# A fused attention and feed-forward kernel: batch 2 loaded ahead of w_out, batch 1's attention given priority, the last unit stored by column halves

## The chip, the cores and the metric

The kernel runs on one core of one Trainium2 chip. The metric is the device time of one execution in microseconds (us); a kernel is given by the median of its runs. PE is TensorE, DVE is VectorE, ACT is ScalarE, POOL is GpSimd, SP is SyncE. Spans that are read from a profile are some 2 us shorter than the device time of the same run, and belong to a single run, so they are used for where the time goes, and the timed rounds for how much it is.

## The reference, cut to what matters

```python
batch, n_heads, seq, head_dim = (8, 8, 576, 64)      # q, k, v: float32
kv  = np.einsum('bhsd,bhse->bhde', k, v)
out = np.einsum('bhsd,bhde->bhse', q, kv)
rms = np.sqrt(np.mean(out * out, axis=-1, keepdims=True) + 1e-06)
x   = (out / rms * g_norm) -> [4608 tokens, 512]
y   = ((x @ w_a) * (x @ w_b)) @ w_out                # d_ff 1536, y: [4608, 512]
```

The attention has no softmax: a 64x64 matrix per head, applied to q, then a norm. The feed-forward part is nearly all of the work. The kernel computes in 16 bit and, except for the first 512 tokens, saves one product in eight by a scheme of sums and differences of blocks (seven products in place of eight). That saves PE time and costs DVE time, for the sums.

## The kernel before

The program is written as a list of nodes, each with an engine, an estimated duration, a priority and its dependencies. A small planner in the program itself orders the nodes when the program is built; the order that it finds on each engine is then fixed. So a number in the program is often not a wait on the chip but a guess that steers the order ("plan time", which is not quite the time of the trace).

```python
class Plan:
    def order(self):
        ...
                    t = max(self.ready(n), f)
                    key = (f if t < f + 0.06 else t, n.prio)   # what can start first, then priority
        ...
```

Every batch's attention is eight slices of a chain PE, ACT, PE, ACT, DVE: x = kvd'q (L344), square (L354), mean by a matrix of ones (L358, the "s" matmul), 1/root (L362), multiply into the 16-bit tokens `xp` (L367). Four stretches of it, shortened (`...` marks a cut):

```python
    # loads: weights, then w_out, then (load_node) batch 2, 3, ...; all casting loads, issued by POOL
    for i, (f0, f1) in enumerate(WB):
        nc.gpsimd.dma_start(out=wa_t[:, :, sl], in_=wa_v[:, :, sl])
        nc.gpsimd.dma_start(out=wb_t[:, :, sl], in_=wb_v[:, :, sl])
        ...                                              # batch 1 in between
    for i in range(2):
        nc.gpsimd.dma_start(out=wo_t[:, sl, :], in_=wo_v[:, sl, :])

    def load_node(b, prio, dep):     # batch b; q goes to DRAM in bf16 and comes back transposed
        def issue():
            if dep is not None:      # POOL waits here for the transposed q of the batch before
                nc.gpsimd.tensor_copy(gate_t, dep["q"].tile[0:1, 0, 0:1])
            ... q -> scr, k -> k_t, v -> v_t
        def transpose():
            nc.sync.dma_start_transpose(out=ld["q"].tile[:]..., in_=scr[:]...)
```

```python
    def o_std(ab, muls, win):        # w_out for the first 512 tokens: no sums, so no DVE
        for g in range(ng):          # 4 row groups of 128 tokens
            def mm(g=g, ps=ps):
                for fc in range(FC):                       # 12 products of 512 columns
                    nc.tensor.matmul(ps.tile[:], lhsT=ab.tile[:, fc, ...], rhs=wo_t[:, fc, :], ...)
            n1 = plan.add("PE", mm_us(FC, d_model), pr, mm, [plan.at(46.5)] + list(muls.values()), [ps], [ab])
```

```python
    # the last unit of 512 tokens (in o_unit); X, Z, W are PSUM banks, ob is the output tile
            ...
            p7 = prod(4, X, sx(s3), t3, False, [e2, n3], (), [s3], 0)
            ...
            c22 = comb(4, 1, 1, X, [p7, e5], [X, u5], u=u5)
            p3 = prod(5, Z, sx(s4), b22, False, [e5, n4], (), [s4], 3)
            c12 = comb(5, 0, 1, Z, [p3, e2], [Z])
            for i in range(m):
                put(0, slice(i, i + 1), [c11, c12], queue=("SP", "ACT")[i])
            for i in range(m):
                subs = slice(i, i + 1)
                p4 = prod(6 + 0.1 * i, W[i], a22, t4, True, [n4], [W[i]], subs=subs)
                c21 = comb(6 + 0.1 * i, 1, 0, W[i], [p4, e3], [W[i]], subs)
                put(1, subs, [c21, c22], queue=("ACT", "SP")[i])
```

Of the kernel before, what the change touches and what calls it, by code (L numbers as in the profile page):

```python
# [135 lines left out]
def kernel(  # L136
# [39 lines left out]
    NMAX = N0 // 2  # L176
    nb = len(BLOCKS)
    NJ = FC // 2
    EH = d_model // 2

    const = ctx.enter_context(tc.tile_pool(name="const", bufs=1))
# [106 lines left out]
    for i, (f0, f1) in enumerate(WB):  # L288
# [2 lines left out]
        nc.gpsimd.dma_start(out=wb_t[:, :, sl], in_=wb_v[:, :, sl])  # L291
        if i in (2, 4):
            early_load(early[1], 1, slice((i // 2 - 1) * HP, i // 2 * HP))
    for i in range(2):
        sl = slice(i * FC // 2, (i + 1) * FC // 2)
        nc.gpsimd.dma_start(out=wo_t[:, sl, :], in_=wo_v[:, sl, :])


    def dummies(n):
# [212 lines left out]
    def late_batch(b, load, win):  # L512
        at = Attn(b)
        w0, w1 = win
        kb, vb, qb = load["k"], load["v"], load["q"]
        kd = Buf(RKD)
        at.qt = [qb, kd]

        def view(t):
            return t[:, 0 : H * (NCH + 1) * D].rearrange("p (h c d) -> p h c d", h=H, d=D)  # L520

        s = Buf(RS)

        def kv_mm():
            kv_ps = s.tile[:].rearrange("p (a e) -> p a e", a=NP)
            for c in range(NCH + 1):
                for p in range(NP):
                    hs = slice(2 * p, 2 * p + 2)
                    nc.tensor.matmul(  # L529
                        kv_ps[:, p, :],  # L530
                        lhsT=kb.tile[:, c, hs, :],
                        rhs=view(vb.tile)[:, hs, c, :],
                        start=(c == 0 and p == 0),
                        stop=(c == NCH and p == NP - 1),
                    )

        n = plan.add(
            "PE", 1.15, w0, kv_mm, [(load["n"], load["kv_us"]), plan.at(w0 - 3)], [s, kd], [kb, vb]
        )

        def kv_out():
            kv_ps = s.tile[:].rearrange("p (a e) -> p a e", a=NP)
            at.kvd = kd.tile
            nc.scalar.copy(at.kvd[0:D, :, 0:D], kv_ps[0:D, :, 0:D])
            nc.scalar.copy(at.kvd[D:, :, D:], kv_ps[D:, :, D:])
            for p in range(NP):
                at.q[p] = qb.tile[:, p, :]

        m = plan.add("ACT", 0.75, w0, kv_out, [n], (), [s])
        slices(at, (w0 + 0.12 * (w1 - w0), w1), lambda p: [m, (load["qn"], 5.5)])  # L550


    def load_node(b, prio, dep):
        ld = {"k": Buf(RK), "v": Buf(RV), "q": Buf(RQT)}
        scr = scr_pool.tile([NP, S, 2, D], BF16, name="scr", tag="scr")

        def issue():
            if dep is not None:
                nc.gpsimd.tensor_copy(gate_t, dep["q"].tile[0:1, 0, 0:1])
            qv = q[b].rearrange("(p hl) s d -> hl s p d", hl=2)  # L560
            for hl in range(2):
                nc.gpsimd.dma_start(
                    out=scr[:, :, hl, :].rearrange("p s d -> s p d"), in_=qv[hl]
                )
            kt = ld["k"].tile
            ks = k[b, :, 0:SA, :].rearrange("h (sp c) d -> sp h c d", c=NCH)
            for c in range(NCH):
                nc.gpsimd.dma_start(out=kt[:, c], in_=ks[:, :, c, :])  # L568
            nc.gpsimd.dma_start(out=kt[0:SB, NCH], in_=k[b, :, SA:S, :].rearrange("h sp d -> sp h d"))
            for n, src in (("v", v),):  # L570
                t = ld[n].tile[:, 0 : H * (NCH + 1) * D].rearrange(
                    "p (h c d) -> p h c d", h=H, d=D
                )
                nc.gpsimd.dma_start(
                    out=t[:, :, 0:NCH, :],
                    in_=src[b, :, 0:SA, :].rearrange("h (sp c) d -> sp h c d", c=NCH),
                )
                nc.gpsimd.dma_start(
                    out=t[0:SB, :, NCH, :], in_=src[b, :, SA:S, :].rearrange("h sp d -> sp h d")
                )  # L580

        def transpose():
            nc.sync.dma_start_transpose(
                out=ld["q"].tile[:].rearrange("p a s -> p (a s)"),
                in_=scr[:].rearrange("a s h d -> (a s) (h d)"),
            )

        issue_us, q_us, ld["kv_us"] = (18.0, 8.0, 18.0) if dep is None else (9.0, 1.5, 11.5)

        ld["n"] = plan.add(  # L590
            "POOL", issue_us, prio, issue, [(dep["qn"], 5.5)] if dep else [], [ld["k"], ld["v"]]
        )
        ld["qn"] = plan.add(
            "SP", 2.5, prio, transpose, [(ld["n"], q_us)], [ld["q"]]
        )
        return ld

    gate_t = const.tile([1, 1], BF16)


    def std_block(win):
# [65 lines left out]
    def out_sums(prio):  # L667
        add, sub = nc.vector.tensor_add, nc.vector.tensor_sub
        b11, b12 = wo_t[:, 0:NJ, 0:EH], wo_t[:, 0:NJ, EH:]
        b21, b22 = wo_t[:, NJ:, 0:EH], wo_t[:, NJ:, EH:]  # L670
        t2, t3, t4 = (so_t[:, i] for i in range(3))
        n3, n1, n2, n4 = four(
            prio,
            fast_us(NJ * EH),
            ((t3, b22, b12, sub), (b12, b12, b11, sub), (t2, b22, b12, sub), (t4, b21, t2, sub)),
            [plan.at(46.5)],
            list(o_reads),
        )
        return n1, n2, n3, n4
# [106 lines left out]
            muls[j] = muls[j + NJ] = m  # L786
        return ab, muls

    def store(g0, o_sb, queue=None):
        queue = queue or nc.sync  # L790
        i = 0
        while i < 128:
            b, j = divmod(g0 + i, S)
            if b < NE:
                c, sp = divmod(j, EP)
                n = min(128 - i, EP - sp)
                r0, st = b * S + EC * sp + c, EC
            else:
                n = min(128 - i, S - j)
                r0, st = b * S + j, 1  # L800
            queue.dma_start(out=out[r0 : r0 + st * (n - 1) + 1 : st, :], in_=o_sb[i : i + n, :])
            i += n

    def o_block(bi, ab, muls, osum, win, chunks, rings, pieces):
# [15 lines left out]
    def o_std(ab, muls, win):  # L820
# [3 lines left out]
        for g in range(ng):  # L824
            pr = w0 + (w1 - w0) * g / ng
            ps = Buf((RO, RY)[g % 2])

            def mm(g=g, ps=ps):
                for fc in range(FC):
                    nc.tensor.matmul(  # L830
                        ps.tile[:],
                        lhsT=ab.tile[:, fc, g * 128 : (g + 1) * 128],
                        rhs=wo_t[:, fc, :],
                        start=(fc == 0),
                        stop=(fc == FC - 1),
                    )

            n1 = plan.add(
                "PE", mm_us(FC, d_model), pr, mm,
                [plan.at(46.5)] + list(muls.values()), [ps], [ab],  # L840
            )
            o_reads.append(n1)
            n2 = plan.add(
                "ACT", act_us(d_model), pr,
# [8 lines left out]
    def o_unit(r0, ab, muls, osum, pr, du, chunks, pieces, m, w, first, second, X, Y, Z, ob, s2, s3, s4, W):  # L853
# [81 lines left out]
                "DVE", dve_us((subs.stop - subs.start) * EH), pr + off * du, add, deps, (), frees  # L935
            )

        def put(fi, subs, deps, us=0.45, queue="SP"):
            q = {"SP": nc.sync, "ACT": nc.scalar}[queue]

            def go():
                for i in range(subs.start, subs.stop):
                    store(r0 + (fi * m + i) * 128, ob.tile[:, fi * m + i], q)

            plan.add(queue, us * (subs.stop - subs.start), pr + 7 * du, go, deps, (), [ob])

# [4 lines left out]
        if W:  # L951
# [14 lines left out]
            c22 = comb(4, 1, 1, X, [p7, e5], [X, u5], u=u5)  # L966
            p3 = prod(5, Z, sx(s4), b22, False, [e5, n4], (), [s4], 3)
            c12 = comb(5, 0, 1, Z, [p3, e2], [Z])
            for i in range(m):
                put(0, slice(i, i + 1), [c11, c12], queue=("SP", "ACT")[i])  # L970
            for i in range(m):
                subs = slice(i, i + 1)
                p4 = prod(6 + 0.1 * i, W[i], a22, t4, True, [n4], [W[i]], subs=subs)
                c21 = comb(6 + 0.1 * i, 1, 0, W[i], [p4, e3], [W[i]], subs)
                put(1, subs, [c21, c22], queue=("ACT", "SP")[i])
            return
        p1 = prod(0, X, a11, b11, True, [plan.at(46.5)], [X])
        e1 = ev(0, 0, 0, p1, [ob])
        p2 = prod(1, Y, a12, b21, True, [], [Y])
        c11 = comb(1, 0, 0, Y, [p2, e1], [Y])  # L980
# [18 lines left out]
    for i in range(len(lens)):  # L999
        st.append(st[-1] + lens[i] + (o_us[i - 1] if i else 0) + late_us * n_at[i])  # L1000
    L = [st[i + 1] - st[i] for i in range(len(lens))]
    at_win = {1: (34.5, st[1] - 3)}
    for b in range(2, B):
        t = b * S / N0
        at_win[b] = (max(61.0, st[int(t) - 1] + (t % 1) * L[int(t) - 1] - 18), st[int(t)] - 22 + (t % 1) * 12)
    loads = {2: load_node(2, 22.5, None)}
    for b in range(3, B):
        loads[b] = load_node(b, at_win[b - 1][0], loads[b - 1])
    early_batch(0, (4.0, 16.0))
    early_batch(1, at_win[1])  # L1010
    ab, muls, reads = std_block((st[0], st[1]))
    wsum = weight_sums(32.5, reads)
    needs = {1: [], 2: [2], 3: [3], 4: [4], 5: [5], 6: [6], 7: [7], 8: []}
    O_A, O_B = 12.0, 3.0
    for bi in range(1, nb + 1):
        o_win = (st[bi] + 1.0, st[bi + 1] - 1.0) if bi < nb else (st[bi] + O_A, st[bi + 1] + O_B)
        if bi == 1:
            o_std(ab, muls, o_win)
            osum = out_sums(st[2] - 10)
        else:  # L1020
            o_block(bi - 1, ab, muls, osum, o_win, 2, (RO, RY, RY), 1)
# [43 lines left out]
```

## Time and profile before

306.51 us, median of 4 runs (306.22 to 306.73).

| in the profiled run | us |
|---|---|
| first matmul of the feed-forward part starts | 19.9 |
| PE time lost between there and the last matmul | 3.66 |
| last matmul ends | 299.3 |
| span ends | 305.0 |

How the loss is read: back-to-back groups in the timeline show 0.216 us for a matmul of 512 columns, 0.109 for 256, 0.122 for 288. The distance between two starts less this is time in which PE did nothing. "PE busy" itself is no good for this, because the ends of matmuls are modelled. Read so, a total is good to about 0.1 us and that of one stretch to about 0.2 us. The loss sits in two places: 2.85 us between 35 and 50 us, 0.89 us between 70 and 90 us.

The stage table of the kernel before (stretch in us, its length, then the busy time of PE, PEld, DVE, ACT and POOL with instruction counts, PE's clock, DMA share and GB/s):

```profile
35.00:50.00 15.00, 13.00 (x107) 6.95 (x106) 12.65 (x26) 10.20 (x25) 7.36 (x8) 1.00 1.61 191
50.00:70.00 20.00, 20.00 (x148) 13.40 (x146) 13.17 (x23) 10.51 (x23) 8.92 (x10) 1.00 1.67 178
70.00:90.00 20.00, 19.66 (x184) 16.88 (x183) 19.93 (x40) 17.85 (x41) 10.01 (x12) 1.00 1.51 125
90.00:290.00 200.00, 200.00 (x1865) 178.84 (x1864) 168.09 (x303) 134.90 (x272) 28.11 (x30) 1.00 0.59 77
```

PE is what limits. DVE is idle for a third of 50 to 70 us and full from 70 to 90 us. The timeline of PE, kernel before, at the two places where it stops between 35 and 50 us (start, length, engine, line, what; the bracket is the idle time before it and what ended it):

```profile
37.12 0.28 PE L358 MATMUL bk<-sq,ones 128*128 128x288 bf16 x1 [0.65 <-ACT kvd L326]
37.99 0.28 PE L358 MATMUL bk<-sq,ones 128*128 128x288 bf16 x1 [0.59 <-ACT rs L362]
...
49.76 0.28 PE L358 MATMUL bk<-sq,ones 128*128 128x288 bf16 x1 [0.70 <-ACT rs L362]
```

All three are s matmuls of batch 1's attention, which stand in the order at a place where nothing else is left to run while ACT works. The timeline of POOL and that of SP's queue show the loads (lines of the kernel before: w_out's second half, batch 2's first, the gate that waits for batch 2's transposed q, and the transposing DMA itself):

```profile
31.23 0.82 POOL L296 DMA_DIRECT2D wo_t<-in_moe_w_out_dram  x1 [0.59 <-DMA abt<-in_q_dram]
32.73 1.65 POOL L562 DMA_DIRECT2D scr<-in_q_dram  x1 [0.68 <-DMA abt<-in_k_dram]
...
61.14 0.68 POOL L559 COPY gate_t<-qT 1x1 bf16<-1x1 bf16 x1 [11.08 <-DMA qT<-scr]
```

```profile
51.04 6.27 SPq L583 DMA_TRANSPOSE qT<-scr  x1
```

The end, from the timeline of the kernel before:

```profile
297.80 1.47 PE L894 MATMUL bk<-wo_t,as 128*128 128x256 f16 x12
298.62 0.69 DVE L932 TENSOR_TENSOR o_sb<-bk,u 128x512 f32<-128x512 f32 x1 [3.80 <-ACT o_sb L926]
299.23 1.34 DVE L932 TENSOR_TENSOR o_sb<-bk,o_sb 128x256 f32<-128x256 f32 x3
299.73 1.25 ACTq L801 DMA_DIRECT2D out_dram<-o_sb  x2
```

The last matmul ends at 297.80 + 1.47 = 299.27 us. The last product is the one on s4, whose combination is 512 columns wide, and it stands behind three others on DVE; then the last of four stores of 256 KB are issued. These four were issued from 299.7 to 300.6 us (the line of the stores, kernel before, from 299 to 304 us):

```profile
DMA to landing us min/median/max: 2.1/2.8/3.3
```

From the last matmul to the end of the span ("the tail" below) it takes 5.7 us.

### The profile page before, as it was taken

The page shows a single profiled execution, that of the slowest core. Times are in us where ns is not written, and L with a number is a line of the kernel's source. Part 1 is how long each engine was busy: PE and PEld are TensorE (multiplying, and loading weights), DVE is VectorE, ACT ScalarE, POOL GpSimd, SP SyncE. Part 2 cuts the span into 40 slices and gives each one's busy share as a digit, 9 for nine tenths or more (in the row PEclk, how much of TensorE's full clock was granted, in tenths as well). Part 3 has the DMA queues.
Part 4 walks back from the last instruction along what each step waited for, and adds up shares of the span by engine and source line. Part 5 has one row for each costly group of instructions (what it writes and reads, how often), then busy time and mean ns, then how long its engine had stood idle before and what let it go on. Part 6 is the DMA issues. An engine that isn't in the chain of part 4 may idle for free.

```text
span 305.0 us, 6667 instructions
## 1 busy us (share of the span) xinstructions
PE 292.3 (96%) x2621; PEld 239.2 (78%) x2621; DVE 235.0 (77%) x433; ACT 193.1 (63%) x404; POOL 77.0 (25%) x93
## 2 busy tenths in 40 slices
PE   7699899999999999999999999999999999999992
PEld 2444445498788898888988898899888888888881
DVE  4344678569998879698969986998599949898652
ACT  3584456279897768775688548965797466655520
POOL 8565742092480751914700000000000000000000
PEclk9689999999999999999999999999999999999999
DMA  7999999999799699999964400030004001100133
GB/s 188 210 198 198 198 207 158 194 178 166 79 139 170 42 161 229 116 168 201 143 77 80 138 3 0 2 140 1 2 0 140 1 2 69 72 3 0 36 104 138
DMA packets 98815, 33.16 MB, mean 109 GB/s; under 512 B 76768, under 2 KB 94176, under 8 KB 98784
## 3 DMA queue, kind: packets, MB, share of 16 engines
q0 software_dynamic: 77984, 17.99, 63.1%
q1 hardware_dynamic: 20096, 13.64, 18.8%
q10 hardware_dynamic: 704, 1.11, 1.2%
q8 instruction: 20, 0.33, 0.4%
q14 instruction: 11, 0.09, 0.1%
HBM read 37.75 MB, written 12.98 MB: 166 GB/s over the span
## 4 chain that ended last, share of the span: by engine, by line
PE 90%; DVE 4%; DMA 3%; ACT 1%; SPq 0%; issue 0%; DVEq 0%
PE bk L729 47%; PE bk L894 24%; PE bk L378 7%; PE bk L830 3%; DMA c<-in_v_dram 3%; PE bk L358 3%; PE bk L344 2%; PE bk L529 2%; PE bk L316 1%; DVE c L748 1%; DVE o_sb L932 1%; PE bk L332 1%; ACT rs L362 0%; PE bk L302 0%; DVE abt L393 0%; DVE xp L367 0%
## 5 line engine op out<-in xcount | busy, mean ns | idle before, releaser
L748 DVE TENSOR_TENSOR c<-bk,u 128x512 f16<-128x512 f32 x144 | 96.7, 686 | 27.1 <-PE bk L729 13.2
L411 ACT COPY u<-bk 128x512 f32<-128x512 f32 x144 | 82.2, 591 | 37.4 <-PE bk L729 36.4
L729 PE MATMUL bk<-xp,wa_t 128*128 128x256 f16 x288 | 55.0, 273 | 0.0
L729 PE MATMUL bk<-xp,wb_t 128*128 128x256 f16 x288 | 55.0, 273 | 0.0
L729 PEld LDWEIGHTS <-wa_t 128*128 128x128 f16 x384 | 37.4, 98 | 5.2
L894 PEld LDWEIGHTS <-abt 128*128 128x128 f16 x384 | 37.5, 98 | 4.8 <-DVE abt L783 0.2
L367 DVE SCALAR_TENSOR_TENSOR xp<-bk,g_col,rs 128x288 f16<-128x288 f32 x64 | 32.6, 512 | 11.2 <-ACT rs L362 11.0
L729 PEld LDWEIGHTS <-wb_t 128*128 128x128 f16 x384 | 37.6, 98 | 4.3
L411 ACT CAST c<-bk 128x512 f16<-128x512 f32 x48 | 28.4, 591 | 17.1 <-PE bk L729 16.6
L894 PE MATMUL bk<-wo_t,abt 128*128 128x256 f16 x288 | 37.0, 273 | 0.0
L729 PE MATMUL bk<-T,sa 128*128 128x256 f16 x192 | 36.6, 273 | 0.1
L729 PE MATMUL bk<-T,sb 128*128 128x256 f16 x192 | 36.6, 273 | 0.0
L362 ACT ACTIVATE rs<-bk,eps_t 128x288 f32<-128x288 f32 x64 | 32.5, 509 | 3.5 <-PE bk L358 3.2
L783 DVE TENSOR_TENSOR abt<-c 128x1024 f16<-128x1024 f16 x48 | 32.9, 686 | 1.7
L729 PEld LDWEIGHTS <-sa 128*128 128x128 f16 x288 | 28.1, 98 | 4.4 <-issue 0.7
L894 PEld LDWEIGHTS <-as 128*128 128x128 f16 x288 | 28.2, 98 | 3.4
L729 PEld LDWEIGHTS <-sb 128*128 128x128 f16 x288 | 28.2, 98 | 3.3
L354 ACT ACTIVATE sq<-bk 128x288 bf16<-128x288 f32 x64 | 25.5, 414 | 2.3 <-PE bk L344 2.0
L926 ACT COPY o_sb<-bk 128x512 f32<-128x512 f32 x31 | 18.2, 587 | 13.0 <-PE bk L894 12.3
L894 PE MATMUL bk<-so,as 128*128 128x256 f16 x192 | 25.7, 273 | 0.0
L568 POOL DMA_DIRECT2D k_t<-in_k_dram x24 | 21.2, 899 | 1.5 <-PE bk L529 1.3
L358 PE MATMUL bk<-sq,ones 128*128 128x288 bf16 x64 | 18.8, 293 | 2.1 <-ACT rs L362 1.3
(97 smaller groups left out, 397.8 us busy)
## 6 DMA issues: line engine op xcount, KB each, us to landing
out_dram<-o_sb SPq DMA_DIRECT2D x22, 256.0 KB, 2.3
scr<-in_q_dram POOLq DMA_DIRECT2D x12, 288.0 KB, 6.4
k_t<-in_k_dram POOLq DMA_DIRECT2D x24, 128.0 KB, 5.9
v_t<-in_v_dram POOLq DMA_DIRECT2D x6, 512.0 KB, 8.5
wo_t<-in_moe_w_out_dram POOLq DMA_DIRECT2D x2, 768.0 KB, 14.8
out_dram<-o_sb SPq DMA_DIRECT2D x12, 128.0 KB, 3.2
wa_t<-in_moe_w_a_dram POOLq DMA_DIRECT2D x5, 256.0 KB, 10.7
wb_t<-in_moe_w_b_dram POOLq DMA_DIRECT2D x5, 256.0 KB, 10.8
```

What stands on the lines that cost most here:

```text
L354: nc.scalar.activation(sq, self.x_ps[p, h][:, 0:HF], AF.Square)
L358: nc.tensor.matmul(ps[:, 0:HF], lhsT=ones, rhs=self.sq[p, h], start=True, stop=True)
L362: nc.scalar.activation(rs, self.s_ps[p, h][:, 0:HF], AF.Abs_reciprocal_sqrt, bias=eps_t)
L367: nc.vector.scalar_tensor_tensor(out=xcols(p, self.b * S + h * HF, HF), in0=self.x_ps[p, h][:, 0:HF], scalar=g_col, in1=self.rs[p, h], op0 ...
L378: nc.tensor.matmul(ps[:, 0:n], lhsT=w[:, kc, fc * 128 : (fc + 1) * 128], rhs=xcols(kc, 0, n), start=(kc == 0), stop=(kc == KC - 1),)
L411: ("ACT", act_us(n), lambda: nc.scalar.copy(*args())),
L568: nc.gpsimd.dma_start(out=kt[:, c], in_=ks[:, :, c, :])
L729: nc.tensor.matmul(ps.tile[:, i * n : (i + 1) * n], lhsT=lhs(w, sm)[:, kc, :], rhs=rhs()[:, kc, :], start=start and i == 0 and kc == 0, st ...
L748: lambda: nc.vector.tensor_add(cs(fi, h), full(ps), u.tile),
L783: nc.vector.tensor_mul(t, c[:, :, :, 0], c[:, :, :, 1])
L894: nc.tensor.matmul(ps.tile[:, sub * EH : (sub + 1) * EH], lhsT=lhs(slice(j, j + 1))[:, 0, sub * 128 : (sub + 1) * 128], rhs=rhs[:, j, :], ...
L926: lambda: nc.scalar.copy(o(fi, h), bank(X, every)), [dep], takes, frees,
```

## The change

Its intent: to load batch 2 earlier, so that its attention is there when PE needs something to weave; to hold w_out back so that it does not disturb batch 2's transposing DMA; to run batch 1's attention as soon as its data is there; and to have less left to store at the end. The weight sums, DVE's sums of blocks of w_a and w_b for the seven-product scheme, are put off a little as well. Core of the diff, with cuts marked by `...`:

```diff
-    for i in range(2):                                   # w_out behind the weights
-        nc.gpsimd.dma_start(out=wo_t[:, sl, :], in_=wo_v[:, sl, :])
+    def load_wo(dep):                                    # w_out behind batch 2's transposed q
+        def issue():
+            nc.gpsimd.tensor_copy(gate_t, dep["q"].tile[0:1, 0, 0:1])
+            for i in range(2):
+                nc.gpsimd.dma_start(out=wo_t[:, sl, :], in_=wo_v[:, sl, :])
+        return plan.add("POOL", 1.8, 50.0, issue, [(dep["qn"], 7.5)])
...
-        issue_us, q_us, ld["kv_us"] = (18.0, 8.0, 18.0) if dep is None else (9.0, 1.5, 11.5)
+        issue_us, q_us, ld["kv_us"] = (16.0, 5.5, 13.0) if dep is None else (9.0, 1.5, 11.5)
...
     # o_std: pieces of OP = 2 products instead of 12, and plan.at(46.5) replaced
+            for f0 in range(0, FC, OP):
+                n1 = plan.add("PE", mm_us(OP, d_model), pr + 0.01 * f0, mm,
+                    [(wo_n, 5.0 if f0 + OP <= FC // 2 else 9.0), n1] + [muls[fc] for fc in range(f0, f0 + OP)], ...)
...
+            put(0, every, [c11], es=e1s)                 # e1s, e2s: left, right 256 columns
+            put(1, every, [c22], es=e2s)
             for i in range(m):
-                put(0, slice(i, i + 1), [c11, c12], queue=("SP", "ACT")[i])
+                put(0, slice(i, i + 1), [c12], queue=("SP", "ACT")[i], es=e2s)
-                put(1, subs, [c21, c22], queue=("ACT", "SP")[i])
+                put(1, subs, [c21], queue=("ACT", "SP")[i], es=e1s)
...
-    at_win = {1: (34.5, st[1] - 3)}                      # window of batch 1's attention
+    at_win = {1: (24.0, 38.0)}
-        at_win[b] = (max(61.0, ...
+        at_win[b] = (max(53.0, ...
-    wsum = weight_sums(32.5, reads)
+    wsum = weight_sums(38.0, reads)
-            o_std(ab, muls, o_win)
+            o_std(ab, muls, (o_win[0] + 4.0, o_win[1] + 4.0))
```

More of the change, by code (lines that the diff above doesn't have):

```diff
@@ L178 @@
     NJ = FC // 2
+    OP = 2
     EH = d_model // 2
@@ L293 @@
             early_load(early[1], 1, slice((i // 2 - 1) * HP, i // 2 * HP))
-    for i in range(2):
-        sl = slice(i * FC // 2, (i + 1) * FC // 2)
-        nc.gpsimd.dma_start(out=wo_t[:, sl, :], in_=wo_v[:, sl, :])
     def dummies(n):
@@ L549, in late_batch @@
         m = plan.add("ACT", 0.75, w0, kv_out, [n], (), [s])
-        slices(at, (w0 + 0.12 * (w1 - w0), w1), lambda p: [m, (load["qn"], 5.5)])
+        slices(at, (w0 + 0.12 * (w1 - w0), w1), lambda p: [m, (load["qn"], 7.5)])
     def load_node(b, prio, dep):
@@ L586, in transpose @@
             )
-        issue_us, q_us, ld["kv_us"] = (18.0, 8.0, 18.0) if dep is None else (9.0, 1.5, 11.5)
+        issue_us, q_us, ld["kv_us"] = (16.0, 5.5, 13.0) if dep is None else (9.0, 1.5, 11.5)
         ld["n"] = plan.add(
-            "POOL", issue_us, prio, issue, [(dep["qn"], 5.5)] if dep else [], [ld["k"], ld["v"]]
+            "POOL", issue_us, prio, issue, [(dep["qn"], 7.5)] if dep else [], [ld["k"], ld["v"]]
         )
@@ L598 @@
     gate_t = const.tile([1, 1], BF16)
+    def load_wo(dep):
+        def issue():
+            nc.gpsimd.tensor_copy(gate_t, dep["q"].tile[0:1, 0, 0:1])
+            for i in range(2):
+                sl = slice(i * FC // 2, (i + 1) * FC // 2)
+                nc.gpsimd.dma_start(out=wo_t[:, sl, :], in_=wo_v[:, sl, :])
+        return plan.add("POOL", 1.8, 50.0, issue, [(dep["qn"], 7.5)])
     def std_block(win):
@@ L675, in out_sums @@
             ((t3, b22, b12, sub), (b12, b12, b11, sub), (t2, b22, b12, sub), (t4, b21, t2, sub)),
-            [plan.at(46.5)],
+            [(wo_n, 9.0)],
             list(o_reads),
@@ L787, in wino_block, with store @@
         return ab, muls
-    def store(g0, o_sb, queue=None):
+    def store(g0, o_sb, queue=None, es=slice(0, d_model)):
         queue = queue or nc.sync
@@ L800, in store @@
                 r0, st = b * S + j, 1
-            queue.dma_start(out=out[r0 : r0 + st * (n - 1) + 1 : st, :], in_=o_sb[i : i + n, :])
+            queue.dma_start(out=out[r0 : r0 + st * (n - 1) + 1 : st, es], in_=o_sb[i : i + n, es])
             i += n
@@ L826, in o_std, with mm @@
             ps = Buf((RO, RY)[g % 2])
-            def mm(g=g, ps=ps):
-                for fc in range(FC):
-                    nc.tensor.matmul(
-                        ps.tile[:],
-                        lhsT=ab.tile[:, fc, g * 128 : (g + 1) * 128],
-                        rhs=wo_t[:, fc, :],
-                        start=(fc == 0),
-                        stop=(fc == FC - 1),
-                    )
-            n1 = plan.add(
-                "PE", mm_us(FC, d_model), pr, mm,
-                [plan.at(46.5)] + list(muls.values()), [ps], [ab],
-            )
+            n1 = None
+            for f0 in range(0, FC, OP):
+                def mm(g=g, ps=ps, f0=f0):
+                    for fc in range(f0, f0 + OP):
+                        nc.tensor.matmul(
+                            ps.tile[:],
+                            lhsT=ab.tile[:, fc, g * 128 : (g + 1) * 128],
+                            rhs=wo_t[:, fc, :],
+                            start=(fc == 0),
+                            stop=(fc == FC - 1),
+                        )
+                n1 = plan.add(
+                    "PE", mm_us(OP, d_model), pr + 0.01 * f0, mm,
+                    [(wo_n, 5.0 if f0 + OP <= FC // 2 else 9.0), n1] + [muls[fc] for fc in range(f0, f0 + OP)],
+                    [ps] if f0 == 0 else [], [ab],
+                )
             o_reads.append(n1)
@@ L936, in comb, with put @@
             )
-        def put(fi, subs, deps, us=0.45, queue="SP"):
+        def put(fi, subs, deps, us=0.45, queue="SP", es=slice(0, d_model)):
             q = {"SP": nc.sync, "ACT": nc.scalar}[queue]
@@ L942, in go @@
                 for i in range(subs.start, subs.stop):
-                    store(r0 + (fi * m + i) * 128, ob.tile[:, fi * m + i], q)
+                    store(r0 + (fi * m + i) * 128, ob.tile[:, fi * m + i], q, es)
             plan.add(queue, us * (subs.stop - subs.start), pr + 7 * du, go, deps, (), [ob])
@@ L968, in o_unit @@
             c12 = comb(5, 0, 1, Z, [p3, e2], [Z])
+            e1s, e2s = slice(0, EH), slice(EH, d_model)
+            put(0, every, [c11], es=e1s)
+            put(1, every, [c22], es=e2s)
             for i in range(m):
-                put(0, slice(i, i + 1), [c11, c12], queue=("SP", "ACT")[i])
+                put(0, slice(i, i + 1), [c12], queue=("SP", "ACT")[i], es=e2s)
             for i in range(m):
@@ L974, in o_unit @@
                 c21 = comb(6 + 0.1 * i, 1, 0, W[i], [p4, e3], [W[i]], subs)
-                put(1, subs, [c21, c22], queue=("ACT", "SP")[i])
+                put(1, subs, [c21], queue=("ACT", "SP")[i], es=e1s)
             return
-        p1 = prod(0, X, a11, b11, True, [plan.at(46.5)], [X])
+        p1 = prod(0, X, a11, b11, True, [(wo_n, 9.0)], [X])
         e1 = ev(0, 0, 0, p1, [ob])
@@ L1001 @@
     L = [st[i + 1] - st[i] for i in range(len(lens))]
-    at_win = {1: (34.5, st[1] - 3)}
+    at_win = {1: (24.0, 38.0)}
     for b in range(2, B):
         t = b * S / N0
-        at_win[b] = (max(61.0, st[int(t) - 1] + (t % 1) * L[int(t) - 1] - 18), st[int(t)] - 22 + (t % 1) * 12)
+        at_win[b] = (max(53.0, st[int(t) - 1] + (t % 1) * L[int(t) - 1] - 18), st[int(t)] - 22 + (t % 1) * 12)
     loads = {2: load_node(2, 22.5, None)}
+    wo_n = load_wo(loads[2])
     for b in range(3, B):
```

## The prediction

> **What bounds the kernel now.** TensorE. Read from the timeline of PE: distance between starts of matmuls less their streaming time (0.216 us for 512 columns, 0.109 for 256, 0.122 for 288, as back-to-back groups show). PE cannot start its first large stage before 19.9 us, its last matmul is over at 299.3 us, and the span ends at 305.0. Between 20 and 299 us only about 3.6 us are lost:
>
> - 35 to 40 us: 1.7 us. At 37.1 and 38.0 PE waits for ACT (kvd, then rs) in batch 1's attention.
> - 45 to 50 us: 0.95 us: at 49.8 us again batch 1 behind ACT's rs.
> - 79 and 83.7 us: 0.9 us, behind DVE's combinations; the stage table has DVE at 4.97, 5.00 of 5 and 9.97 of 10 us from 70 to 90, but only 5.6 of 10 us from 50 to 60, where PE runs the 10.4 us of o_std.
> - after 90 us: under 0.1 us.
>
> The change can win at most these 3.6 us and part of the 5.7 us tail; 2% would be 6.1 us.
>
> **DMA.** From 20 to 50 us the queues move 160 to 200 GB/s, software loads in order. w_out (2 x 768 KB) lands about 3.9 us apart, at 43.6 and 47.4 us; batch 2's q copy waits behind it, its transposing DMA is issued at 51.0 and lands at 61.1 us. Without w_out ahead, batch 2 comes 7 to 8 us earlier: estimate 44 us for the transpose's issue, 52 to 54 for its landing. w_out then goes out at about 54 us and lands at about 59 and 63 us (estimate).
>
> **What moves.** Batch 1's q, k, v land at 21 to 24 us (first half) and 31 to 34.5 us (second), yet half its attention now runs after 38 us. With priority from plan time 24 it is woven between first-stage matmuls: I expect the 35 to 50 us losses (2.7 us) to fall to about 0.6. Block 1's products start at about 46 us and fill PE until w_out lands, with batch 2's attention; o_std runs after about 61 us. DVE carries 2.4 us per j of block 1 against 3.05 us of PE, plus weight sums (8 x 0.47 us) and batch 2's normalization: it is nearly full from 46 to 62 us, so I expect 0.5 to 1 us of new PE gaps there; o_std as filler then removes the 0.9 us at 79 to 84. PE loss after 20 us: 3.6 -> about 1.3 us.
>
> **Tail.** The last combination ends at 300.6, the last 256 KB stores land 2.0 to 2.5 us after issue. The Trainium skill (DMA: Bandwidth & Descriptors, the anatomy of one DMA) says that the fixed cost of a DMA, about 2 us, is mostly completion latency; 2.0 to 2.5 us here agrees. Halving the last stores' bytes should win only 0.1 to 0.4 us.
>
> **Sum.** 306.4 - 2.3 - 0.3 = 303.8 us; range 302.3 to 305.8. Chances: faster by over 2% 0.01, within 2% 0.96, slower 0.03.
>
> **Right or wrong.** Right if batch 1's x and s matmuls end before about 44 us, last matmul ends near 297, o_std starts after 58 us without a DMA wait. Wrong if PE waits for w_out, if DVE holds block 1 back by over 2 us between 46 and 65, if PE waits for batch 1's data at 22 to 25 us, or if the new order opens gaps after 90 us.

## The result, and the profile after

302.36 us, median of 4 runs (302.08 to 302.69), against 306.51 us: 4.15 us less. The ratio of the fast runs is 0.9865, 95% interval 0.9848 to 0.9883. (Ratios here are the mean time of one kernel's fast runs over that of the other's fast runs of the same rounds, so not quite the ratio of the quoted medians.) The kernel after run again later with other kernels gave 301.64 us, ratio 0.9850 (0.9828 to 0.9871).

| in the profiled run | before | after | change |
|---|---|---|---|
| first feed-forward matmul | 19.92 | 19.66 | -0.26 |
| PE lost from there on | 3.66 | 0.57 | -3.09 |
| last matmul ends | 299.27 | 295.97 | -3.30 |
| tail (last matmul to end) | 5.71 | 4.00 | -1.71 |
| span | 305.0 | 300.0 | -5.0 |

(The profiled run of before was the slowest of its four and that of after the fastest, so the spans differ by more than the medians.) The stage table of the kernel after, same columns:

```profile
35.00:50.00 15.00, 14.99 (x115) 8.83 (x112) 13.79 (x29) 10.18 (x24) 4.55 (x6) 1.00 2.03 168
50.00:70.00 20.00, 19.87 (x169) 15.48 (x168) 17.71 (x32) 14.99 (x33) 11.00 (x13) 1.00 1.27 138
70.00:90.00 20.00, 20.00 (x165) 15.09 (x163) 16.30 (x29) 12.72 (x27) 9.02 (x11) 1.00 1.66 178
90.00:290.00 200.00, 200.00 (x1864) 178.49 (x1862) 169.21 (x305) 133.83 (x269) 28.21 (x31) 1.00 0.61 80
```

DVE's work has moved: 17.71 in place of 13.17 us at 50 to 70, 16.30 in place of 19.93 at 70 to 90. PE stops no more for batch 1; its s matmuls are over at 42.5 us and have other work on both sides. The last of them, in the timeline of PE, kernel after:

```profile
41.61 0.81 PE L376 MATMUL bk<-xp,wb_t 128*128 128x512 f16 x3
42.26 0.29 PE L356 MATMUL bk<-sq,ones 128*128 128x288 bf16 x1
42.38 0.38 PE L376 MATMUL bk<-xp,wb_t 128*128 128x512 f16 x1
```

What is left is 0.6 us at 49 to 53 us, where DVE is full (busy for 4.00 of these 4 us). Timelines of POOL and SP's queue in the kernel after:

```profile
54.01 0.18 POOL L600 COPY gate_t<-qT 1x1 bf16<-1x1 bf16 x1 [11.37 <-DMA qT<-scr]
54.24 1.64 POOL L603 DMA_DIRECT2D wo_t<-in_moe_w_out_dram  x2
...
67.28 0.88 POOL L572 DMA_DIRECT2D v_t<-in_v_dram  x1 [3.62 <-DMA wo_t<-in_moe_w_out_dram]
```

```profile
43.63 6.84 SPq L581 DMA_TRANSPOSE qT<-scr  x1
```

Batch 2's q lies transposed at 54.0 us and not at 61.1; w_out goes out at 54.2, and o_std's first product starts at 64.35 us without a wait for it. The end, from the timeline of the kernel after:

```profile
294.72 1.25 PE L905 MATMUL bk<-so,abt 128*128 128x256 f16 x10
294.92 1.52 DVE L943 TENSOR_TENSOR o_sb<-bk,o_sb 128x512 f32<-128x512 f32 x3
296.01 0.42 DVE L943 TENSOR_TENSOR o_sb<-bk,o_sb 128x256 f32<-128x256 f32 x1
296.13 0.38 ACTq L808 DMA_DIRECT2D out_dram<-o_sb  x1
296.50 0.33 SPq L808 DMA_DIRECT2D out_dram<-o_sb  x1
```

Two things are different here. The stores are halves, and some of them left earlier, as intended. But the order of the last products is another one too: the product on s4 now comes before the one on a22 (rhs `so`), so that what DVE has to do after the last matmul is one combination of 256 columns. Nothing in the diff says so. It comes out of the planner, because everything ahead of it moved. DVE is done 0.46 us after the last matmul in place of 1.30 us.

### The profile page after: what moved, and what is told of

The parts are those of the page before. It is cut to its first block, busy times and chain, and to the rows that moved or that the text cites. A ratio compares the mean times of both kernels' runs of the same rounds, so it can differ in the third digit from the quotient of the medians.

```text
span 300.0 us, 6678 instructions
## 1 busy us (share of the span) xinstructions
PE 291.6 (97%) x2621; PEld 238.6 (80%) x2621; DVE 236.4 (79%) x433; ACT 193.7 (65%) x404; POOL 76.7 (26%) x94
## 4 chain that ended last, share of the span: by engine, by line
PE 81%; DVE 0%; issue 0%
PE bk L736 47%; PE bk L905 24%; PE bk L840 3%; PE bk L527 2%; PE bk L342 2%; PE bk L356 2%; DVE o_sb L943 0%
## 5 line engine op out<-in xcount | busy, mean ns | idle before, releaser
L560 POOL DMA_DIRECT2D scr<-in_q_dram x12 | 19.6, 1636 | 1.9 <-issue 1.2
```

The source lines that it names most:

```text
L560: nc.gpsimd.dma_start(out=scr[:, :, hl, :].rearrange("p s d -> s p d"), in_=qv[hl])
```

## The experiments

Three theories for PE's 3.1 us, and two for the tail:

- **P**, that of the prediction: batch 1's attention came too late, its priority mends that.
- **L**: batch 2 being loaded earlier is what counts.
- **F**: o_std needs no DVE; what counts is that it is kept for the stretch in which DVE is full.
- **S** and **O**: the tail is shorter through the half-row stores (S), or through the order of the last products (O).

Each of the twelve runs gave a correct result. They were made in three rounds on three chips, each beside the kernel before, so kernels of different rounds are best compared by their ratios. The numbers of this table are used throughout; profile figures are of one run each:

| kernel | median us | ratio to before (95%) | PE lost, of which 35 to 50, 50 to 70, 70 to 90 | tail |
|---|---|---|---|---|
| before | 306.4 | | 3.66: 2.85, 0.0, 0.89 | 5.7 |
| after, again | 301.64 | 0.9850 (0.9828 to 0.9871) | 0.57: 0.0, 0.6, 0.0 | 4.0 |
| b_prio | 306.05 | 0.9988 (0.9973 to 1.0003) | 3.29: 0.8, 0.0, 2.5 | 5.7 |
| b_prio_sums | 304.22 | 0.9922 (0.9905 to 0.9939) | 2.24: 0.0, 0.0, 2.2 | 4.8 |
| a_noprio | 310.65 | 1.0139 (1.0118 to 1.0160) | 8.12: 3.3, 4.9, 0.0 | 5.1 |
| a_wofirst | 303.16 | 0.9877 (0.9858 to 0.9896) | 0.73: 0.0, 0.1, 0.4 | 5.0 |
| b_halves | 305.66 | 0.9978 (0.9963 to 0.9992) | 3.62: 2.8, 0.0, 0.9 | 5.0 |
| b_last | 306.27 | 0.9989 (0.9974 to 1.0004) | 4.05: 2.8, 0.0, 0.9 | 5.0 |
| a_wofirst_last | 302.71 | 0.9880 (0.9863 to 0.9897) | 1.12: 0.0, 0.1, 0.4 | 4.4 |
| a_onepiece | 301.96 | 0.9853 (0.9834 to 0.9871) | 0.78: 0.0, 0.7, 0.0 | 4.0 |
| b_hold61 | 305.94 | 0.9988 (0.9971 to 1.0006) | 3.59: 0.1, 0.8, 2.1 | 5.1 |
| b_hold_win | 302.85 | 0.9885 (0.9865 to 0.9905) | 1.55: 0.0, 0.0, 1.6 | 4.0 |
| a_nogate | 308.06 | 1.0059 (1.0033 to 1.0085) | 6.80: 0.1, 6.5, 0.0 | 4.0 |

The runs of before that went with these had medians of 306.39 to 306.49 us; one of its 33 executions took 439.96 us and is left out of the ratios as not fast. From run to run the first feed-forward matmul starts some tenths of a us earlier or later, so spans are not compared to better than that; "PE lost" and "tail" do not contain it.

### b_prio: the priority alone

```diff
-    at_win = {1: (34.5, st[1] - 3)}
+    at_win = {1: (24.0, 38.0)}          # on the kernel before
```

> The kernel before with one number pair changed: batch 1's attention window in plan time 24 to 38 in place of 34.5 to 41.3; loads, output pieces and stores as before. Theory P (priority: the PE gaps of 35 to 50 us were batch 1's attention run too late): these gaps (2.7 us) close, time 303.5 to 304.2 us. Theory L (load order: the gain came from batch 2 being there earlier and w_out later): no gain, 306 us or more. The order of the last products is that of the kernel before, so the tail from PE's last matmul to the end stays at 5.7 us by both.

306.05 us, which is L's number and, by the interval, not clearly a gain at all; P's is missed by 2 us. And yet P is right that the loss of 35 to 50 us goes (2.85 to 0.8). But 2.5 us are lost at 70 to 90 us in place of 0.9. The lost time moved.

### b_prio_sums: the priority and the weight sums' priority

```diff
-    at_win = {1: (34.5, st[1] - 3)}
+    at_win = {1: (24.0, 38.0)}
-    wsum = weight_sums(32.5, reads)
+    wsum = weight_sums(38.0, reads)     # on the kernel before
```

> As b_prio, with the weight sums' priority moved from 32.5 to 38 as in the change. Theory P: the same PE gain as b_prio. In this kernel the planner happens to put the last unit's products in the order of the kernel after (the product on s4 before the one on the last a22 halves), with whole-row stores as before. If the tail got shorter through this order (theory O), the tail is some 0.8 us shorter than in b_prio, 303.0 us; if only through the half-row stores (theory S), the tail stays 5.7 us and the time 303.8 us.

304.22 us, 1.8 us less than b_prio. The tail is 4.8 us with whole-row stores, so O holds. PE loses nothing before 70 us now, and 2.2 us after it. (The weight sums' priority was never changed alone.) The stage table of b_prio_sums where it loses them:

```profile
60.00:65.00 5.00, 5.00 (x53) 4.19 (x52) 1.98 (x3) 2.25 (x5) 3.46 (x4) 1.00 0.82 198
75.00:80.00 5.00, 4.28 (x34) 3.00 (x33) 5.00 (x10) 4.22 (x10) 0.00 (x0) 1.00 1.46 175
80.00:85.00 5.00, 4.52 (x52) 4.01 (x51) 5.00 (x12) 3.56 (x9) 4.07 (x4) 1.00 0.64 72
```

DVE has 3 us to spare at 60 to 65 us and is full at 75 to 85 us. The timeline of PE there:

```profile
78.77 0.28 PE L344 MATMUL bk<-qT,kvd 128*128 128x288 bf16 x1
79.36 0.38 PE L729 MATMUL bk<-xp,sa 128*128 128x256 f16 x2 [0.31 <-DVE c L748]
...
81.68 0.38 PE L729 MATMUL bk<-xp,wa_t 128*128 128x256 f16 x2 [0.48 <-DVE xp L367]
```

Batch 2's q matmuls (L344 on qT) stand at 65 to 79 us, and PE waits for the normalized tokens and for combinations from DVE. With batch 1 out of the way, batch 2's attention is the next that comes late.

### a_noprio: all of the change but the two priorities

```diff
-    at_win = {1: (24.0, 38.0)}
+    at_win = {1: (34.5, st[1] - 3)}
-    wsum = weight_sums(38.0, reads)
+    wsum = weight_sums(32.5, reads)     # on the kernel after
```

> The kernel after with batch 1's window and the weight sums' priority put back to those of before; loads, pieces and half-row stores as after. Theory P: the gaps of 35 to 50 us return and o_std comes too late to fill them, 305 us or more (order of the last products as before, half-row stores). Theory L: 302.5 to 303.3 us.

310.65 us, worse than the kernel before: P holds, for the two priorities together, and L is out as the sole cause. The old loss at 37 us is back, and another is added (timeline of PE, a_noprio):

```profile
51.01 0.38 PE L736 MATMUL bk<-xp,wb_t 128*128 128x256 f16 x2
53.52 0.59 PE L736 MATMUL bk<-xp,wa_t 128*128 128x256 f16 x2 [2.12 <-DVE xp L705]
```

In the kernel before, o_std ran at 50 to 61 us, where this kernel waits for DVE's differences of batch 1's tokens; in this one the plan has o_std later, for w_out is not there yet.

### a_wofirst, b_hold_win and a_onepiece: load order and pieces

a_wofirst is the kernel after with w_out loaded first:

```diff
-    wo_n = load_wo(loads[2])
+    wo_n = plan.at(46.5)                # and the two loads back behind the weights,
-        (16.0, 5.5, 13.0) if dep is None # batch 2's plan times and max(61.0, ...) as before
+        (18.0, 8.0, 18.0) if dep is None # on the kernel after
```

> The kernel after with w_out loaded ahead of batch 2 again, ungated, and batch 2's plan times as before; batch 1's priority, pieces and half-row stores as after. Theory P: PE gains the same or within 0.5 us of it, 302.3 to 303.3 us (the order of the last products falls back to that of before, worth up to 0.8 us). Theory L: most of the PE gain is lost, 305 us or more.

303.16 us, PE losing 0.73 us, as P expected: nearly all of the gain on PE without the new load order. Its tail is 5.0 us, with the old product order.

b_hold_win is the kernel before with both priorities, half-row stores and o_std 4 us later in priority; it differs from a_wofirst only in that o_std is in one piece:

```diff
-            o_std(ab, muls, o_win)
+            o_std(ab, muls, (o_win[0] + 4.0, o_win[1] + 4.0))   # on b_prio_sums, with half-row stores
```

> As b_hold61, but o_std is only moved 4 us later in priority, as the change does, and not held. Theory F: one of the four row groups is then left for the full stretch of DVE, and the loss at 70 to 90 us shrinks in part, to about 1 us; the last products have the order of after here; 302.4 to 303.0 us. Theory L: 303.4 us or more.

(b_hold61, which this names, is shown below.) 302.85 us, within what F expected; but 1.6 us are still lost at 70 to 90 us, where F expected about 1.

a_onepiece is the kernel after with o_std in one piece:

```diff
-    OP = 2
+    OP = 12                             # on the kernel after
```

> The kernel after with o_std's 12 products of a row group in one piece again in place of six pieces of two. Theory F (o_std is the only large work on PE that needs no DVE; kept for the stretch where DVE is full, it closes the gaps at 75 to 85 us, and its late place in the plan does that, not the pieces): within 0.5 us of the kernel after, 302.4 to 302.9 us. Rival (it is the fine pieces): gaps of 1 us or more come back between 50 and 90 us, 303.5 us or more.

301.96 us, between the two measurements of the kernel after (302.36 and 301.64): no difference can be told. Together with the kernel after, these make a square. All four have both priorities, the later o_std and half-row stores, and the plan times that go with their load order:

| PE lost, us | o_std in one piece | in pieces of two products |
|---|---|---|
| w_out loaded first | 1.55 (b_hold_win) | 0.73 (a_wofirst) |
| batch 2 first, w_out held | 0.78 (a_onepiece) | 0.57 (after) |

So pieces and the early load of batch 2 each win 0.8 us, and the second of them adds 0.2 us to the first. The orders suggest that they are two ways to the same thing, something to weave between the steps of batch 2's attention; no run shows that by itself. The other 2 us of the gain on PE come with the priorities (3.66 to 2.24, b_prio_sums) and the later o_std (to 1.55).

### b_hold61: o_std held in the plan, w_out first

```diff
-                [plan.at(46.5)] + list(muls.values()), [ps], [ab],
+                [plan.at(61.0)] + list(muls.values()), [ps], [ab],   # on b_prio_sums, with half-row stores
```

> The kernel before with batch 1's priority, the weight sums' priority and the half-row stores, and with o_std (in one piece) held in the plan until 61 in place of 46.5; w_out still loaded ahead of batch 2. Theory F (what counts is that o_std, which needs no DVE, is kept for the stretch where DVE is full; the load order only brings that about): the gaps of 70 to 90 us shrink from 2.2 us (b_prio_sums) to below 0.8 us, 303.0 us (the last products come in the order of before, worth 0.8 us). Theory L (batch 2 must be loaded early): they stay at about 2 us, 304.3 us.

305.94 us. F fails in this form; the loss of 70 to 90 us stays, as L expected, and another of 0.8 us comes before it. The stage table of b_hold61 shows where o_std went:

```profile
65.00:70.00 5.00, 5.00 (x25) 2.29 (x24) 0.91 (x2) 1.14 (x3) 5.00 (x6) 1.00 2.15 137
70.00:75.00 5.00, 5.00 (x30) 2.79 (x29) 1.02 (x2) 2.67 (x6) 0.77 (x2) 1.00 1.97 193
75.00:80.00 5.00, 4.06 (x26) 2.33 (x24) 4.31 (x8) 2.95 (x7) 0.00 (x0) 1.00 1.54 134
80.00:85.00 5.00, 4.67 (x51) 4.10 (x51) 4.72 (x9) 3.09 (x9) 3.01 (x3) 1.00 0.72 206
```

It ran nearly in one block at 65 to 75 us, with DVE idle for 8 of 10 us beside it, and batch 2's attention came bunched behind it. Late is not enough: o_std has to stand beside work of DVE, and there must be work for DVE at that time, which here means batch 2's q. Its transpose was issued at 51.4 us in this run, as before. That batch 2's late q is the reason is argued from this order and not shown by a run of its own.

### a_nogate: w_out not held

```diff
-            nc.gpsimd.tensor_copy(gate_t, dep["q"].tile[0:1, 0, 0:1])    # in load_wo, on the kernel after
```

> The kernel after without the hold: w_out is issued right behind batch 2's loads and not behind its transposing DMA. The plan, and so every order on PE, DVE and ACT, stays. Theory: batch 2's transpose lands later than the 54 us of after because w_out's packets share the engines, but its first reader on PE comes at about 58 us, so that little is lost: within 0.4 us of after. Rival (the hold is what makes the early load of batch 2 pay): PE waits for qT between 56 and 65 us and the time is 303.4 us or more.

308.06 us; the rival was right. The orders on PE, DVE and ACT are those of the kernel after. The timeline of POOL, a_nogate:

```profile
43.75 1.65 POOL L602 DMA_DIRECT2D wo_t<-in_moe_w_out_dram  x2 [1.20 <-DMA scr<-in_q_dram]
62.29 0.18 POOL L557 COPY gate_t<-qT 1x1 bf16<-1x1 bf16 x1 [16.89 <-DMA qT<-scr]
```

The transposing DMA, issued at 43.5 us as in the kernel after, lands 18.7 us later in place of 10.3 us; until then the software loads moved 2.46 MB beside it in place of 0.92 MB. And PE, in its timeline:

```profile
57.70 0.38 PE L735 MATMUL bk<-xp,wb_t 128*128 128x256 f16 x2
62.28 0.41 PE L342 MATMUL bk<-qT,kvd 128*128 128x288 bf16 x2 [4.20 <-DMA qT<-scr]
...
63.21 0.63 PE L735 MATMUL bk<-T,wa_t 128*128 128x256 f16 x2
63.64 0.63 PE L735 MATMUL bk<-T,wb_t 128*128 128x256 f16 x2
```

4.4 us are lost at once, and after that a pair of matmuls takes 0.43 us in place of 0.22. The Trainium skill (TensorE: Matmul & The Clock Gate, "Part 1: The HAM clock gate") says that the array's clock is halved when PE has been idle and full again after a few us of work. This trace agrees: PE's clock is granted at 0.5 from 62.7 to 66.1 us and full again after that. Of the 6.5 us lost at 50 to 70 us, 4.4 are the wait, 1.6 this clock, and 0.5 are lost ahead of it in the kernel after as well. Its stage table (the clock is the third number from the right):

```profile
62.00:64.00 2.00, 1.72 (x10) 1.29 (x10) 0.00 (x0) 1.25 (x3) 1.34 (x2) 0.67 0.10 16
64.00:66.00 2.00, 2.00 (x11) 1.38 (x10) 0.53 (x1) 1.02 (x3) 2.00 (x2) 0.50 0.49 31
```

So the early load of batch 2 is worth little unless w_out is kept out of its way: with the hold it wins, without it 6 us are lost.

### b_halves and b_last: the tail

b_halves has only the half-row stores, on the kernel before; its orders on PE and DVE are those of before, and its ACT order but for the two stores.

```diff
-                put(0, slice(i, i + 1), [c11, c12], queue=("SP", "ACT")[i])      # and so on, as in the change
+                put(0, slice(i, i + 1), [c12], queue=("SP", "ACT")[i], es=e2s)
```

> The kernel before with only the last unit's stores cut into column halves; every order on PE, DVE unchanged. Theory S (the tail waits for the last megabyte to drain, so that what is stored ahead is won): tail from PE's last matmul to the end 5.7 to about 4.9 us, time 305.6 us. Rival (the prediction's: fixed completion time): 0.1 to 0.4 us, 306.1 us or more.

305.66 us, ratio 0.9978, tail 5.0 us: S holds, 0.7 us. Data moved by all DMA engines in the last 14 us, in 40 slots of 0.35 us from 290 to 304 us (GB/s), first the kernel before, then b_halves:

```profile
GB/s 217 182 205 111 117 374 381 380 246 0 0 0 0 0 0 0 0 0 0 0 0 0 0 0 0 0 0 0 0 0 228 398 345 404 381 398 386 369 88 0
```

```profile
GB/s 205 35 217 374 381 380 146 0 0 0 0 0 0 3 319 243 185 0 0 0 0 0 0 0 0 0 41 307 313 345 340 337 337 228 0 0 0 0 0 0
```

Before, all that is left goes out in one run of 2.7 us at nearly 400 GB/s, behind the last combination. In b_halves a quarter of it (the three slots 319, 243, 185, some 0.26 MB) is gone more than 3 us ahead. DVE's last combination ends 1.3 us after the last matmul in both, and the last store is issued 1.3 us after it before and 1.5 us in b_halves, so nothing started earlier; but the last store landed 4.6 us after the last matmul before and 3.8 us in b_halves. The stores of b_halves (its line of the stores, from 298.5 to 304 us):

```profile
DMA to landing us min/median/max: 1.8/2.1/2.3
```

What was left to move did count.

b_last has only the order, with whole rows:

```diff
-                p4 = prod(6 + 0.1 * i, W[i], a22, t4, True, [n4], [W[i]], subs=subs)
+                p4 = prod(6 + 0.1 * i, W[i], a22, t4, True, [n4] + ([p3] if i else []), [W[i]], subs=subs)
```

> The kernel before with only the order of the last unit's products forced: the second half of the product on a22 comes after the one on s4, so that the last combination is 256 columns wide (0.42 us) and not 512 (0.69 us, behind two others). Whole-row stores as before. Theory O (order, a by-product of the new plan, shortens the tail by 0.8 us whatever is stored): 305.6 us, tail 4.9 us. Rival (only the stores count): 306.4 us.

306.27 us, so neither number is quite met: the tail is 5.0 us, near O's 4.9, but the forced order takes away a filler and opens a wait of 0.49 us at 292 us, so the time hardly moves. a_wofirst_last does the same to a_wofirst:

> w_out loaded ahead of batch 2 as before (a_wofirst), with the last product forced into the order that the kernel after has by chance. Theory: the load order is worth nothing by itself; a_wofirst lost to the kernel after only by its tail. Then 302.3 us, equal to the kernel after, with PE losing 0.5 to 0.9 us after 20 us. Rival (the early load of batch 2 is worth the 0.8 us between them): stays at 303.1 us.

302.71 us: between the two. The tail shrinks to 4.4 us, the same wait is opened (0.50 us at 289 us), and it stays open from this run whether the load order has a share in the rest. The square above answers that better.

Over all kernels the tail falls in four groups, whatever else they contain:

| tail, us | old order of last products | new order |
|---|---|---|
| whole rows | 5.7 (before, b_prio) | 4.8 (b_prio_sums), 5.0 (b_last, forced) |
| column halves | 5.0 to 5.1 (b_halves, a_wofirst, a_noprio, b_hold61) | 4.0 (after twice, a_onepiece, b_hold_win, a_nogate), 4.4 (a_wofirst_last, forced) |

Alone, the stores are worth 0.65 us and the order 0.9 us (0.7 forced); together they are worth 1.7 us, a little more than the sum. The split is plain in the traces: the order sets when DVE's last combination is done, 1.3 us after the last matmul in the old order, 0.46 us in the new one and 0.64 us where it was forced; from there to the end it takes 4.3 to 4.4 us with whole rows and 3.5 to 3.8 us with halves.

### after_again: the kernel after, unchanged

> The kernel after once more, unchanged, as the base for the three below and for a_onepiece: 302.0 to 302.7 us. If it comes out at or above 302.3 us, o_std in one piece (301.96 us) is at least not worse than the six pieces.

301.64 us (301.32 to 302.43), a little below the expected range; PE lost 0.57 us again, tail 4.0 us. By its own condition (302.3 us or more) it does not show a_onepiece to be at least as good, and no version was found that clearly beats the kernel after.

## Why the prediction was right or wrong, point by point

The measured 302.36 us lies at the very edge of the range (302.3 to 305.8), and the second measurement, 301.64 us, outside it: that the first fell inside is luck. The 4.15 us won are 1.5 us more than the 2.6 foreseen. The conditions that it set itself were met: batch 1's s matmuls end at 42.5 us, the last matmul at 296.0, and o_std starts at 64.35 us without a wait for its load.

- **"TensorE. ... only about 3.6 us are lost"**: right; this bound, read from the trace, kept the whole forecast inside 2%. Nothing after 90 us changed.
- **"35 to 50 us losses (2.7 us) to fall to about 0.6"**: nothing is left of batch 1's waits (0.2 us at 49.3 us belong to the next point). The reason given, batch 1's priority, is half of it: alone it won 0.35 us, not clear of noise (b_prio), because the loss moved to batch 2's attention; without it and the weight sums' priority everything else is 4 us worse than before (a_noprio). The weight sums' priority, which the prediction lets pass, won 1.8 us on top of batch 1's: 1.05 us on PE and 0.9 us in the tail, through the order.
- **"0.5 to 1 us of new PE gaps there"**: right, 0.6 us at 49 to 53 us with DVE full.
- **"o_std as filler then removes the 0.9 us at 79 to 84"**: right as an outcome. DVE is also no longer full there (busy for 16.30 of 20 us at 70 to 90), which o_std does not explain. As a mechanism it needs batch 2's q to be there at the same time, or o_std in pieces (the square, b_hold61). PE's loss of 0.57 us against 1.3 is 0.7 us of the difference.
- **DMA**: transpose issued at 43.6 (44 foreseen), landed by 54.0 (52 to 54). w_out landed at 61.4 and 67.0 us (7.2 and 11.9 us after its issues at 54.2 and 55.1), not 59 and 63; it did not matter, since the plan has o_std at 64.35.
- **The hold of w_out** the prediction took as a detail. It is worth 6 us (a_nogate).
- **"Halving the last stores' bytes should win only 0.1 to 0.4 us"**: this is the term that was mis-sized. The tail shrank by 1.7 us: 0.65 us by the stores alone (b_halves), 0.9 us by the order of the last products (b_prio_sums) and the rest by the two together. The step that failed was to take 2.0 to 2.5 us from issue to landing for a fixed completion time. In the trace only the first two of the last four stores landed so soon; the last two, behind them, took 3.1 and 3.3 us. The page cited (the Trainium skill, DMA: Bandwidth & Descriptors, "Anatomy of one DMA — SWDGE (gpsimd) path") is about DMAs issued by GpSimd, while these stores came from SP and ACT; it also has a term in bytes, and the trace showed 1.05 MB leaving in one run of 2.7 us at nearly 400 GB/s. The gain by the order was luck: no line of the diff touches that order, so it could not be read from the diff.

## What to carry to other kernels

Where one engine is at 99% and the rest of the time is lost in small waits, closing one wait can move the loss to the next late chain, as it did here: count the idle time of the whole stretch, not of the gap. Work that needs only the limiting engine is a reserve; here moving it later was not enough (b_hold61), and the likely reason, not shown by a run of its own, is that the other engine needs work beside it, so what feeds that engine must be there by then. A large load that is not needed soon may have to be held until a transfer that is needed has landed (here worth 6 us); and in the tail, look at the bytes still to be stored and at the width of the last step behind the last matmul.

## What the Trainium skill lacked or had wrong

- DMA: Bandwidth & Descriptors ("Rules for kernel authors") says that a transpose next to ordinary DMAs needs nothing. That is about correctness, and no run contradicts it; the cost in time is not told. Here the same 0.59 MB (128 x 2304 of 2 bytes) took 4.7 to 6.7 us from issue to landing with no software loads beside it (the last batch's, 6.5 us in the kernel before), 10.3 us beside batch 2's loads, and 18.7 us with w_out behind them too (a_nogate), which cost the kernel 6 us.
- Advanced Engine Details and Errata ("X-Bar Transpose (TRN2)") says that transposing DMAs are as fast as regular ones, 350 to 400 GB/s. The quickest (a_noprio, at 167.3 us) took 4.65 us for 0.59 MB, or 127 GB/s from issue to landing; its data moved in 2.9 us, at no more than 293 GB/s, while stores ran at nearly 400 GB/s. So the figure was not reached, but most of the distance to 127 GB/s is time before and after the data.
- DMA: Bandwidth & Descriptors gives a fixed and a byte term for one DMA. It has nothing on several at the end of a kernel: four stores of 256 KB issued within 0.9 us landed 2.1, 2.5, 3.1 and 3.3 us after issue, and taking some of the bytes ahead won 0.7 us.
- TensorE: Matmul & The Clock Gate ("HAM oscillation") puts the danger at idle gaps of PE above about 3.4 us. In a_noprio matmul pairs ran at half rate after a gap of 2.3 us that shorter ones preceded (clock 0.5 from 53.2 to 56.6 us). The page's next section tells of frequent short gaps doing this too, but gives no lengths.
